# Gate and value products of a SwiGLU block in three float32r passes over split operands, in place of float32 products

## The chip, the cores and the metric

The kernel runs on one core of one Trainium2 chip. The metric is the device time of one execution in microseconds, the median of the runs; lower is better. Engine names are those of the profile: PE (TensorE matmuls), PEld (its weight loads), DVE (VectorE), ACT (ScalarE), POOL (GpSimd), SP (SyncE, which here issues most DMA transfers).

## The reference

A causal depthwise convolution of seven taps (softmax weights, one set for each of eight heads of 24 channels) over `x` of 8 x 4096 x 192, then a SwiGLU feed-forward block with RMS norm over the 32768 tokens, all in float32. The feed-forward weights arrive as float64.

```python
out = np.einsum('hk,bskhg->bshg', softmax(weight), windows_of(x_pad))      # K = 7 taps, causal
x = out.reshape(B * S, D)                                                  # 32768 x 192
rms = np.sqrt(np.mean(x * x, axis=-1, keepdims=True) + 1e-06)
xn = x / rms * rms_g
g = xn @ w_gate                                                            # 192 -> 1536
silu = g * (1.0 / (1.0 + np.exp(-g)))
val = xn @ w_val                                                           # 192 -> 1536
return (silu * val @ w_out).astype(np.float32)                             # 1536 -> 192
```

## The kernel before

**Tiling.** The tokens go in 32 pairs of 1024 (`PT`), each of two groups of `T` = 512. The 192 channels are three blocks of 64 (`KP`), the 1536 features twelve blocks of 128 (`FC`), in four units (`NU`) of three (`NF`). A normalized input tile `xb` holds each block of 64 channels twice: the lower 64 partitions meet the gate's weights, the upper 64 those of the value. A product of one channel block with one feature block and one token group is two matmul instructions of 64 x 512, one per half of the array, which run at the same time into two PSUM banks. All products are in float32.

**Gate and value.** Pair 0 uses plain products (`plain`, matmul on L1052): 2 groups x 12 feature blocks x 3 channel blocks = 72. From pair 1 on a scheme with sums of operands needs 60 in place of 72: 15 per unit. `XSUM` (L67) gives eleven sums of inputs (`x_sum`, L701, into `xc`), `WSUM` (L71) nineteen sums of weights, made once (`w_sums`, L361, on POOL). `CHAIN` (L749) lists the products; `Unit.product` (L792) issues them on L794. Results are carried from bank to bank: `Unit.do` (L800) has copies out (S), copies into a new bank (F; `copy`, L741, with L743 on ACT and L745, L747 on DVE), additions (D, N, C, R, L810 to L826), the silu on ACT (G, L839) and the product of silu and value (M, L846, on POOL or DVE). The hidden blocks go into `ht`.

**Output.** The product with `w_out` uses seven forms of a Strassen kind (`OUTS`, L865) with six steps each: 42 steps per pair, each of six tiles of 128 x 32 weights, four of which run side by side in the columns of the array (`Pair.tile`, L933, matmul on L934). The sums of hidden blocks that the forms need are made on POOL (`Pair.sum`, L954, instructions on L962), 24 per pair. Pair 0 has plain output products (`outer`, L1086, matmul on L1093). DVE turns the results in 32 x 32 blocks (L949) and SP stores them.

**Ahead of the pair.** The convolution of pair p + 2 runs during pair p, in three parts of 512 columns that stand in PSUM banks (`part_tap`, L460: a first tap on ACT, L468, six on DVE, L476). Then square, sum, power and scaling (`square` to `scale`, L489 to L532), a way through DRAM that turns the tile (`place`, L657, SP) and the fetch into `xb` (`fetch_part`, L690, SP).

**Order.** From pair 1 on the order of all instructions is written out by hand in `ORDER` (L90). A word such as `p2` emits the next two steps of PE; `VR1.0.0` is an action on DVE, with A for ACT, G for POOL, D for DMA issues; a word that ends in `-` belongs to the pair before. Each engine, and SP's queue too, takes its instructions in this order. The start, up to the end of pair 0, is laid out by `START`, `LATER` and times given to `put` (L1178 to L1261).

Of the kernel before, what the change touches and what calls it, by code (L numbers as in the profile page):

```python
# [11 lines left out]
F32 = mybir.dt.float32  # L12
AF = mybir.ActivationFunctionType
# [6 lines left out]
def kernel(  # L20
# [45 lines left out]
    XOP = (5, 6, 9, 0, 15, 14, 4, 7, 13, 10, 2, 11, 12, 8, 3)  # L66
    XSUM = (  # L67
        (0, 1, 4), (1, 2, 6), (2, 0, 6), (9, 3, 5), (3, 3, 8), (4, 7, 15), (5, 4, 15), (6, 5, 7),
        (7, 0, 1), (8, 1, 2), (9, 8, 15),
    )  # L70
    WSUM = (  # L71
        (9, "sub", 5, 2), (9, "sub", 9, 8), (10, "sub", 1, 4), (10, "add", 7, 10),
        (11, "sub", 1, 8), (7, "sub", 7, 11), (11, "sub", 4, 11), (12, "add", 1, 6),
        (4, "sub", 12, 4), (5, "sub", 5, 4), (5, "add", 3, 5), (13, "sub", 2, 6),
        (13, "add", 0, 13), (14, "sub", 3, 12), (3, "sub", 6, 3), (0, "add", 0, 3),
        (3, "sub", 3, 2), (6, "neg", 6, 6), (8, "neg", 8, 8),
    )
    WAT = (7, 9, 2, 0, 1, 4, 5, 11, 14, 6, 10, 12, 8, 3, 13)

    SPAN = 1509
    ORDER = (  # L90
        "p2 GX4- VT11- p2 AS40.0.0 GX9- AS40.1.0 p2 AF0.1.0 AF0.0.0 p2 VC.0.0 Dload- p2",
        "VC.1.0 AS41.0.0 VS41.1.0 p2 AS00.1.0 VS00.0.0 p2 Vbc- VD5.0.0 Gmul- p2 VD5.1.0",
        "AS42.0.0 VS42.1.0 AS51.1.0 p2 AS51.0.0 VR1.0.0 p2 VR1.1.0 VR0.0.0 p2 AF2.0.0 VN.1.0",
        "AG0.0.0 p2 VR0.1.0 AF3.0.0 Dplace- AF3.1.0 p2 GM0.1.0 VR2.0.0 p2 VR2.1.0 AS44.1.0",
        "AS44.0.0 VR5.1.0 p2 AG2.0.0 VR3.0.0 p2 GM2.1.0 AS40.0.1 VR3.1.0 AS40.1.1 p2 VR5.0.0",
        "AG4.0.0 p2 VM4.1.0 AF0.0.1 AG5.0.0 VF0.1.1 p2 AG1.0.0 VS41.0.1 GM5.1.0 p1 AS41.1.1",
        "p1 VC.0.1 AG3.0.0 p1 VC.1.1 p1 GM3.1.0 VS00.0.1 p2 AS42.0.1 VS42.1.1 AS00.1.1 GS3.0",
        "p2 VD5.0.1 p1 VD5.1.1 p1 AS51.0.1 GS1.0 VR1.0.1 AS51.1.1 p2 VR1.1.1 AF2.0.1 GS3.1 p2",
        "AF2.1.1 VR0.0.1 AG1.0.1 p1 VR0.1.1 p1 GM1.1.1 VF3.0.1 AF3.1.1 p2 AG0.0.1 VR2.0.1 p1",
        "VR2.1.1 p1 GM0.1.1 AS44.0.1 AS44.1.1 VR5.0.1 p2 GS2.0 VR5.1.1 p2 AS40.0.2 VR3.1.1",  # L100
        "AS40.1.2 p1 VR3.0.1 GM1.1.0 p1 AG4.0.1 AG3.0.1 p1 VM4.1.1 p1 GM3.1.1 VF0.0.2 AF0.1.2",
        "p2 AS41.0.2 VS41.1.2 p1 AG5.0.1 p1 VC.0.2 GM5.1.1 p1 VC.1.2 p1 AS00.0.2 AS00.1.2 p2",
        "GS1.1 AS42.1.2 AS42.0.2 p2 VD5.0.2 GS3.2 p1 VD5.1.2 p1 AS51.0.2 VR1.0.2 AS51.1.2 p2",
        "GS2.1 VR1.1.2 AF2.0.2 p2 AF2.1.2 VR0.0.2 GS1.2 AG1.0.2 p1 VR0.1.2 p1 AG0.0.2 VF3.0.2",
        "GM1.1.2 p1 AF3.1.2 p1 VR2.0.2 AG2.0.1 p1 VR2.1.2 p1 AS44.0.2 GM2.1.1 AS44.1.2 p2",
        "VR3.0.2 AG2.0.2 GS2.2 p1 VR3.1.2 p1 AS40.0.3 VR5.0.2 AS40.1.3 p2 GM2.1.2 AG4.0.2",
        "VR5.1.2 AG3.0.2 p1 VM4.1.2 p1 AF0.0.3 GM0.1.2 p2 AF0.1.3 VS41.0.3 AS41.1.3 p2",
        "GM3.1.2 AG5.0.2 VC.0.3 p1 VC.1.3 p1 AS00.1.3 GS3.3 AS00.0.3 p2 VS42.0.3 AS42.1.3 p2",
        "GS1.3 VD5.0.3 p1 VD5.1.3 p1 AS51.0.3 GM5.1.2 VR1.0.3 AS51.1.3 p2 VR1.1.3 AF2.0.3 p2",
        "GS2.3 AF2.1.3 VR0.0.3 AG1.0.3 p1 VR0.1.3 p1 GS4.2 VF3.0.3 AF3.1.3 p2 AS44.0.3",  # L110
        "VS44.1.3 p1 GM1.1.3 p1 VR5.1.3 p1 VR5.0.3 p1 Acv0_1 VR3.0.3 AG5.0.3 p1 Vcv1_1 Acv0_2",
        "GM5.1.3 p2 VR3.1.3 AG0.0.3 p2 AG3.0.3 Vcv1_2 DfetA GS3.4 p1 AG4.0.3 p1 VR2.0.3 p2",
        "Acv0_0 Vcv2_2 GM3.1.3 p2 VM4.1.3 p2 Vcv2_1 Ac1 GS3.5 p1 AG2.0.3 p1 Vcv3_1 p2 GS1.4",
        "Vcv3_2 p2 Vcv1_0 p2 GS2.4 p1 Vcv2_0 p2 Vcv4_1 p1 As7 GS1.5 DfetB Dst0- p1 VR2.1.3 p2",
        "Vcv5_1 p1 GM0.1.3 p1 Vcv3_0 p2 Vcv6_1 p1 GS2.5 p1 Vcv4_0 p2 Vcv4_2 GS4.0 p2 Vcv5_0",
        "p2 GS4.1 p1 Vcv6_0 p2 Vcv5_2 Ac2 p1 GX0 p1 Vcv6_2 p2 VM2.1.3 Asq p2 GS4.4 p4 VX3 p1",
        "GS4.3 p4 VX6 p1 GX2 p2 VC22 p2 VX1 p2 GS4.5 VT22 p2 Vred p2 GX8 p3 GX7 p2 VC21 p2",
        "VT21 Gpow p2 VX5 p2 VX10 p2 VT12 p1 Dst1 p1",
# [15 lines left out]

    def load_heads(p, b, t0):

        t = x_sb[p] = xs.tile([P, TB + HALO, GS], F32, name="xh")
        if p == 1:
            nc.gpsimd.tensor_copy(out=t[:, 0, 0:1], in_=x0[:, NJ + HALO - 1, 0:1])

        def get(dst, tb, h, dims, r):
            row = x[b, t0 + tb * TB + r - HALO, h * GS :]
            src = bass.AP(
                tensor=row.tensor, offset=row.offset, ap=[dims, [D, TB + HALO - r], [1, GS]]
            )
            nc.sync.dma_start(out=dst, in_=src)

        first = 0
        if t0 == 0:
            nc.gpsimd.memset(t[0:H, 0:HALO, :], 0.0)  # L150
            get(t[0:H, HALO:, :], 0, 0, [GS, H], HALO)
            first = 1
        for h in range(H):
            get(t[first * H + h :: H], first, h, [TB * D, P // H - first], 0)
# [28 lines left out]
    ps = [psum.tile([P, T], F32, name=f"ps{i}") for i in range(8)]  # L183
# [17 lines left out]
    NW = 15  # L201
    wf = [cst.tile([P, NW, P], F32, name=f"wf{u}") for u in range(NU)]
# [13 lines left out]
    def load_in(u, q):  # L216
# [9 lines left out]
    NT = 11  # L226
    few = NT - 6
    early = work.tile([P, 3, NJ * D], F32, name="early")
    kept = [early[:, i].rearrange("p (j d) -> p j d", d=D) for i in range(3)]
    kept = itertools.cycle(kept)  # L230
    flat3 = early[:].rearrange("p i n -> p (i n)")
    NK = FC // 2
    held = [flat3[:, k * T : (k + 1) * T] for k in range(9)]
    more = work.tile([P, 2, T], F32, name="more")
    diff, both, rest = held[0:NK], held[NK:], [more[:, i] for i in range(2)]
    nw = 4 * (FC // 2) * (D // 2)
    tw = x0[:].rearrange("p j d -> p (j d)")[:, 0:nw].rearrange(
        "p (i k d) -> p i k d", i=4, k=FC // 2
    )
    tl6 = [work.tile([P, 3, T], F32, name=f"tls{i}") for i in range(2)]  # L240
    tiles = [work.tile([P, T], F32, name=f"tile{i}")[:] for i in range(few)]
    room = [t[:].rearrange("p j d -> p (j d)") for t in tl6]
# [102 lines left out]
    xb = cst.tile([P, 2, KP, T], F32, name="xb")  # L345
    NX = len({s[0] for s in XSUM})
    xc = cst.tile([P, NX, T], F32, name="xc")
    spare = xc[:].rearrange("p i t -> p (i t)")
# [12 lines left out]
    def w_sums(u):  # L361
        t = wf[u]
        for i, (d, op, a, b) in enumerate(WSUM):
            if op == "neg":
                nc.gpsimd.tensor_scalar(
                    out=t[:, d, :], in0=t[:, a, :], scalar1=-1.0, scalar2=None, op0=ALU.mult
                )
            else:
                nc.gpsimd.tensor_tensor(
# [3 lines left out]
            if i % 4 == 3:  # L373
                yield
        yield


    def convert_in(u):

# [930 lines left out]
```

## Time and profile before

| | |
|---|---|
| time, median of 3 runs | 2594.28 us (2593.07 to 2600.1) |
| span of the profiled execution, first to last instruction | 2591.8 us |
| instructions | 60798 |
| matmul records, all / on L794 / on L934 | 23872 / 7440 / 15624 |
| gate and value of one pair, output of one pair (chain) | 51.92 us, 27.44 us |
| plain products of pair 0 (L1052), output of pair 0 (L1093) | 62.17 us, 31.31 us |
| granted TensorE clock | 1.000 |
| HBM read, written | 83.84 MB, 49.55 MB |

How to read it: the span is cut into groups of instructions by line, engine and tile, each with its count, busy time and mean duration. Records of one engine can overlap, and then a group's busy time divided by its count is less than the mean. The chain of waits is followed back from the last instruction: at each step to what released it, or to the instruction before it on its engine. A stretch of the chain on one line with no other line between is time in which that engine never waited.

### The profile page before, as it was taken

To read this page: it belongs to the slowest core of one execution; us is meant where nothing else is said; L and a number is where in the kernel's file an instruction comes from. 1 tells how busy PE (TensorE), PEld (TensorE's weight loads), DVE (VectorE), ACT (ScalarE), POOL (GpSimd) and SP (SyncE) were. 2 spreads that over 40 slices of the span, in tenths; PEclk is the share of its full clock that TensorE was granted. 3 is DMA by queue.
4 is the path that set the end of the run, shared out by engine and by line. 5 is a ranking of instruction groups with operands and counts; after the bars stand their busy time and mean duration, and the time that the engine had idled before them with its cause. 6 is when DMAs were issued, how large, how long until landed. Compare 5 with 4: busy or idle time off the path is not lost.

```text
span 2591.8 us, 60798 instructions
## 1 busy us (share of the span) xinstructions
PE 2580.5 (100%) x23872; PEld 1778.0 (69%) x23872; DVE 2298.8 (89%) x3681; ACT 1553.5 (60%) x2825; POOL 2190.6 (85%) x1791
## 2 busy tenths in 40 slices
PE   9999999999999999999999999999999999999999
PEld 6876666767667666676666676666766666766667
DVE  8898898988989989989889899899898898988975
ACT  6576555675555765556755557655566555676554
POOL 4898888988889888898888898888988888988877
PEclk9999999999999999999999999999999999999999
DMA  6232332222331323322223313233222233122210
GB/s 145 57 57 33 63 64 52 44 45 51 63 63 38 57 33 64 63 49 47 45 51 64 62 38 55 36 63 63 46 49 45 52 63 58 37 56 40 50 44 14
DMA packets 512397, 137.33 MB, mean 53 GB/s; under 512 B 483950, under 2 KB 486510, under 8 KB 512110
## 3 DMA queue, kind: packets, MB, share of 16 engines
q1 hardware_dynamic: 508364, 132.53, 27.2%
q8 instruction: 187, 3.06, 0.5%
q10 hardware_dynamic: 3746, 0.92, 0.2%
q14 instruction: 100, 0.82, 0.1%
HBM read 83.84 MB, written 49.55 MB: 51 GB/s over the span
## 4 chain that ended last, share of the span: by engine, by line
PE 99%; DVE 0%; issue 0%; DVEq 0%
PE ps L794 62%; PE ps L934 33%; PE ps L1052 2%; PE ps L1093 1%; DVE xb L647 0%; DVE wf L338 0%; DVE xc L333 0%; DVE o_sb L949 0%; DVE xc L298 0%; DVE xc L303 0%; DVE xc L306 0%; DVEq L1305 0%
## 5 line engine op out<-in xcount | busy, mean ns | idle before, releaser
L794 PE MATMUL ps<-xc,wf 64*128 64x512 f32 x4960 | 1214.0, 591 | 0.0
L794 PEld LDWEIGHTS ps<-xc,wf 64*128 64x128 f32 x4960 | 681.3, 186 | 375.3 <-issue 176.7
L794 PE MATMUL ps<-xb,wf 64*128 64x512 f32 x2480 | 679.7, 591 | 0.0
L743 ACT ACTIVATE tile<-ps 128x512 f32<-128x512 f32 x678 | 391.1, 593 | 389.0 <-PE ps L794 295.3
L743 ACT ACTIVATE tls<-ps 128x512 f32<-128x512 f32 (+1 forms) x562 | 323.5, 589 | 438.6 <-PE ps L794 222.0
L846 POOL TENSOR_TENSOR ht<-ht,tile 128x512 f32<-128x512 f32 x329 | 418.9, 1275 | 141.0 <-ACT tile L839 65.2
L794 PEld LDWEIGHTS ps<-xb,wf 64*128 64x128 f32 x2480 | 353.9, 187 | 182.9 <-issue 93.6
L846 POOL TENSOR_TENSOR ht<-ht,tls 128x512 f32<-128x512 f32 x260 | 330.6, 1274 | 86.4 <-ACT tls L839 38.8
L743 ACT ACTIVATE ps<-ps 128x512 f32<-128x512 f32 (+1 forms) x589 | 336.0, 580 | 87.9 <-PE ps L934 32.6
L962 POOL TENSOR_TENSOR early<-ht 128x512 f32<-128x512 f32 x279 | 354.8, 1276 | 4.9
L476 DVE SCALAR_TENSOR_TENSOR ps<-xh,tp,ps 128x512 f32<-128x512 f32 x450 | 320.3, 748 | 4.0 <-ACT ps L468 1.8
L934 PE MATMUL ps<-ht,wo_sb 128*32 128x128 f32 (+2 forms) x5208 | 318.5, 380 | 0.0
L934 PEld LDWEIGHTS ps<-ht,wo_sb 128*32 128x32 f32 x5208 | 233.9, 110 | 81.7 <-POOL ht L846 23.5
L934 PE MATMUL ps<-ht,x 128*32 128x128 f32 (+2 forms) x4464 | 250.7, 379 | 0.0
L826 DVE TENSOR_TENSOR tile<-ps,tile 128x512 f32<-128x512 f32 x349 | 237.4, 683 | 10.2 <-PE ps L794 5.0
L962 POOL TENSOR_TENSOR ht<-ht 128x512 f32<-128x512 f32 x186 | 239.0, 1285 | 4.9
L826 DVE TENSOR_TENSOR ht<-ps,tile 128x512 f32<-128x512 f32 x328 | 222.5, 680 | 6.5 <-ACT tile L743 6.5
L934 PEld LDWEIGHTS ps<-ht,x 128*32 128x32 f32 x4464 | 184.3, 110 | 61.3
L839 ACT ACTIVATE tile<-tile 128x512 f32<-128x512 f32 x349 | 214.5, 625 | 0.0
L826 DVE TENSOR_TENSOR ht<-ps,tls 128x512 f32<-128x512 f32 x292 | 199.0, 681 | 6.8 <-ACT tls L743 3.6
L826 DVE TENSOR_TENSOR tls<-ps,tls 128x512 f32<-128x512 f32 x271 | 184.9, 683 | 17.0 <-PE ps L794 13.8
L934 PE MATMUL ps<-early,x 128*32 128x256 f32 (+2 forms) x3348 | 196.0, 379 | 0.0
(149 smaller groups left out, 3278.1 us busy)
## 6 DMA issues: line engine op xcount, KB each, us to landing
xb<-xd SPq DMA_DIRECT2D x120, 384.0 KB
xd<-yn SPq DMA_DIRECT2D x244, 96.0 KB
xh<-in_x_dram SPq DMA_DIRECT2D x192, 105.0 KB
out_dram<-o_sb SPq DMA_DIRECT2D x122, 96.0 KB
out_dram<-o_sb SPq DMA_DIRECT2D x60, 128.0 KB
xh<-in_x_dram SPq DMA_DIRECT2D x56, 98.4 KB
out_dram<-o_sb SPq DMA_DIRECT2D x122, 32.0 KB
ht<-in_moe_w_gate_dram SPq DMA_DIRECT2D x12, 192.0 KB
```

The source lines that it names most:

```text
L476: nc.vector.scalar_tensor_tensor(out=dst, in0=xk, scalar=w, in1=at, op0=ALU.mult, op1=ALU.add)
L743: nc.scalar.activation(out=dst, in_=src, func=AF.Copy, scale=float(s))
L794: nc.tensor.matmul(out=self.new(v, h, True) if first else self.old(v, h), lhsT=wf[self.u][HALF[h], WAT[i], :], rhs=x_op(XOP[i])[HALF[h]], ...
L826: nc.vector.tensor_tensor(out=self.hv(v) if h else t[:], in0=self.old(v, h), in1=t[:], op=plus(s))
L839: nc.scalar.activation(out=t[:], in_=src[:], func=AF.Silu)
L846: engine[eng].tensor_tensor(out=self.hv(v), in0=src, in1=t[:], op=ALU.mult)
L934: nc.tensor.matmul(out=self.bank(b)[i * Q : (i + 1) * Q, at : at + n], lhsT=left, rhs=cols, start=fresh, stop=True, skip_group_check=True, ...
L962: engine[eng].tensor_tensor(out=dst, in0=a, in1=b, op=op)
L1052: nc.tensor.matmul(out=bank(h, bks[h])[:], lhsT=wf[u][HALF[h], AT[h][k] * NF + f, :], rhs=xb[HALF[h], g, k, :], start=(k == 0), stop=(k == ...
L1093: nc.tensor.matmul(out=bank(h, bks[h])[:, w : w + D], lhsT=hts[f // NF][HALF[h], g, f % NF, j * P : (j + 1) * P], rhs=wo_sb[HALF[h], f, :] ...
```

## The change

Gate and value from pair 1 on are computed otherwise; the output's 42 steps stay.

- **Split operands.** Each weight operand is split once into three parts: the high bits (a mask, `HIGH`), 4096 times the rest, and their difference divided by 1 + 2^-12 and rounded to float32r. Each input operand is split per pair: rounded to float32r (`n`), the rest (`l`), and 2^-12 times the first less the second (`d`). The sum of the three products of like parts is the whole product, but for a factor 1 / (1 + 2^-12), which `factor` puts right in the norm. So each product is three passes of float32r matmuls, two instructions each (`Pair.product`).
- **Which products.** Feature blocks go in six block pairs j. For j = 0, 2, 4 (`FORM`) a Strassen form needs 7 products for two of the three channel blocks and 4 plain ones for the third: 11. For j = 1, 3, 5 there are 12 plain ones. In all 69 per pair of token groups. Four sums of inputs (`x_sum`) replace eleven.
- **Pair 1** has 72 plain float32 products, since the split weights are made during it and before it (`prepare`, words `W` in `FIRST`; it writes them to DRAM, `wd`).
- **Weights from DRAM.** The split weights do not stay in SBUF. A ring of ten slots of 128 x 384 is filled by SP, 45 loads of 196.6 KB per pair; a slot is loaded anew after the last product that uses it (`ring_load`).
- **PSUM** is taken as four double banks (`duo`), so that one instruction of 1024 columns copies gate and value at once (f1, f3, f4, f5).
- **The rest of the order.** Sums of hidden blocks: 18 of 24 on DVE, six on POOL (before, all on POOL). The product of silu and value is always on DVE. The convolution of pair p + 1 runs during pair p, in SBUF, with 1536 columns an instruction. Some DMA issues go to ACT's queue. `ORDER` is new, with `FIRST` for the window of pair 1; a word with `+` belongs to the next pair. `LINE` is the order of PE's steps: a word such as `P1.0` or `Aa.1` is a gate and value product of block pair 0 or 1, `o4.5` an output step.

```diff
-    XSUM = (
...
-    WSUM = (
...
+    SPLIT = 2.0**-12
+    HIGH = 0xFFFFF000
+    FORM = (1, 0, 1, 0, 1, 0)
...
+    ORDER = (
+        "p12- As7- Acv0+ Ac2- Vl.1 Vcv1+ p10- Gh4.0- Vh4.5- Vh4.1- Vcv2+ Vh4.3- Vcv3+ VC22-",
+        "Vcv4+ Gh4.4- VT22- Vl.0 p8- Gh4.2- VT11- VC21- VT21- p3- p1 Af1.0 p1 VT12- p1 Vcv5+",
+        "p5 Af3.0 Aga.0 Vcv6+ Vma.0 p1 Vf4.0 Gl.4 p5 Asq+ Aga.1 Agb.1 Vred+ Vmb.1 Vma.1 p1",
+        "Gpow+ Vf5.0 Agc.0 p2 Vmc.0 Vbc+ p1 Agc.1 Agd.0 Vmd.0 p2 Agb.0 Gmul+ p1 Vmc.1 Vmb.0",
...
+        "Vd.1+",
+    )
...
+    LINE = (
+        "P1.0 Aa.1 P5.0 Q1.0 P2.0 Ba.1 P6.0 Ea.1 Ab.1 Eb.1 Bb.1 Q2.0 P7.0 P3.0 Ac.1 Ec.1 Bc.1",
...
+        "Bd.5 o1.0 o1.3 o1.1 o1.5 o1.4 o1.2 o7.0 o7.2 o7.1 o7.4 o7.3 o7.5 o2.5 o6.3 o6.4 o6.5",
...
+    duo = [psum.tile([P, 2, T], F32, name=f"ps{i}") for i in range(4)]
+    ps = [duo[i % 4][:, i // 4, :] for i in range(8)]
...
+        s = (1.0 + SPLIT) ** -2 if p > 1 else 1.0
...
+    def prepare(o):
...
+        high = parts[:, 0]
+        nc.vector.tensor_scalar(
+            out=high.bitcast(U32), in0=src.bitcast(U32), scalar1=HIGH, scalar2=None,
+            op0=ALU.bitwise_and,
+        )
+        nc.scalar.activation(out=w4, in_=src, func=AF.Copy, scale=1.0 / SPLIT)
+        yield
+        nc.vector.scalar_tensor_tensor(
+            out=parts[:, 1], in0=high, scalar=-1.0 / SPLIT, in1=w4, op0=ALU.mult, op1=ALU.add
+        )
+        yield
+        nc.gpsimd.tensor_tensor(out=e, in0=parts[:, 1], in1=high, op=ALU.subtract)
+        yield
+        nc.scalar.activation(
+            out=parts[:, 2].bitcast(F32R), in_=e, func=AF.Copy, scale=1.0 / (1.0 + SPLIT)
+        )
+        yield
+        nc.sync.dma_start(out=wd_of[o][:, js], in_=st.rearrange("p (j x) -> p j x", j=NP)[:, js])
...
+    def ring_load(slot):
+        n = next(taken)
+        q, (j, o) = 2 + n // len(pieces_of), pieces_of[n % len(pieces_of)]
...
+        r = (j * NW + o) * P
+        nc.sync.dma_start(out=ring[0][:, slot, :], in_=wd[r : r + P, :])
...
+    def split(act, g, eng):
+        src, high = operand(g), split_of(g, 0)
+        e = engine.get(eng)
+        if act == "n":
+            copy(eng, high.bitcast(F32R), src)
+        elif act == "l":
+            e.tensor_tensor(out=split_of(g, 1).bitcast(F32R), in0=src, in1=high, op=ALU.subtract)
+        else:
+            nc.vector.scalar_tensor_tensor(
+                out=split_of(g, 2).bitcast(F32R), in0=high, scalar=1.0 + SPLIT, in1=src,
+                op0=ALU.mult, op1=ALU.subtract,
+            )
...
+        def product(self, w, j):
...
+            for q in range(3):
+                left = ring[0][:, slot, q * P : (q + 1) * P].bitcast(F32R)
+                right = split_of(g, q)[:, i, :].bitcast(F32R)
                 for h in range(2):
+                    nc.tensor.matmul(
+                        out=self.both(j, c)[:, h, :], lhsT=left[HALF[h]], rhs=right[HALF[h]],
+                        start=(first and q == 0), stop=True, skip_group_check=True,
+                    )
+            left_of[key] -= 1
+            if left_of[key] == 0:
+                ring_load(slot)
...
+            if act == "f1":
+                self.open((j, "b"), True)
+                copy(eng, self.both(j, "b"), self.both(j, "a"))
+            elif act == "f3":
+                copy(eng, s5, self.both(j, "c"))
+            elif act in ("f4", "f5"):
...
+                nc.vector.tensor_tensor(
+                    out=self.both(j, c), in0=self.both(j, "b"), in1=s5, op=ALU.add
+                )
+            elif act[0] == "g":
...
+                nc.scalar.activation(
+                    out=tt[:, t, :], in_=self.both(j, c)[:, 0, :], func=AF.Silu
+                )
+            elif act[0] == "m":
...
+                nc.vector.tensor_tensor(
+                    out=self.hv(j, "abcd".index(c)), in0=self.both(j, c)[:, 1, :],
+                    in1=tt[:, t, :], op=ALU.mult,
+                )
+            elif act[0] == "h":
+                self.h_sum(int(act[1]), j, eng)
```

Words of `ORDER` that the prediction names: `ga` to `gd` silu, `ma` to `md` its product with the value, `h1` to `h4` sums of hidden blocks, `cv0` to `cv6` taps, `sq`, `red`, `pow`, `bc`, `mul` the norm, `pl` the way into DRAM, `ft` the fetch of x, `ld` loads of x, `st` stores, `s7`, `c1`, `c2`, `C22`, `C21` carries of output banks, `T11` to `T22` the turns.

## The prediction, on record before the changed kernel ran

> **What bounds the kernel now.** I read the chain of waits first, then its stretch of two steady pairs, then busy time by stretch. On the page, the chain is PE and almost nothing else:
>
> ```profile
> span 2591.8 us, 60798 instructions
> PE 2580.5 (100%) x23872; PEld 1778.0 (69%) x23872; DVE 2298.8 (89%) x3681; ACT 1553.5 (60%) x2825; POOL 2190.6 (85%) x1791
> PE ps L794 62%; PE ps L934 33%; PE ps L1052 2%; PE ps L1093 1%; DVE xb L647 0%; DVE wf L338 0%; DVE xc L333 0%; DVE o_sb L949 0%; DVE xc L298 0%; DVE xc L303 0%; DVE xc L306 0%; DVEq L1305 0%
> ```
>
> PE works without a gap: L794 (gate and value) and L934 (output) alternate. The chain in order of time (start, length, what), at the beginning and in two later pairs:
>
> ```profile
> 32.40 62.17 PE ps L1052 x271
> 94.58 31.31 PE ps L1093 x380
> 126.37 51.72 PE ps L794 x239
> 178.09 27.44 PE ps L934 x337
> ```
>
> ```profile
> 1157.98 51.92 PE ps L794 x240
> 1209.90 27.44 PE ps L934 x337
> 1237.34 51.92 PE ps L794 x240
> ```
>
> A pair is 51.92 + 27.44 = 79.36 us. The 51.92 are 60 products of 512 columns, 0.865 us each, both halves of the array at once. L1052 agrees: 72 products in 62.17 us, 0.863 each. The model of the whole is 126.4 (start and pair 0) + 79.2 (pair 1) + 30 x 79.36 + 4.9 (from the last matmul to the end) = 2591.3 against a span of 2591.8. The median of the runs, 2594.28, is 2.5 us above that span; I add these 2.5 at the end.
>
> How far are the others from being the bound? Busy time by stretch (PE, PEld, DVE, ACT, POOL, clock, DMA share, GB/s):
>
> ```profile
> 1158.00:1209.90 51.90, 51.90 (x244) 32.83 (x248) 45.58 (x75) 41.50 (x77) 41.70 (x33) 1.00 0.23 35
> 1209.90:1237.30 27.40, 27.40 (x507) 21.00 (x506) 25.95 (x40) 6.60 (x11) 26.79 (x23) 1.00 0.37 83
> 43.00:46.00 3.00, 3.00 (x17) 1.44 (x14) 3.00 (x4) 0.90 (x2) 2.40 (x4) 1.00 1.07 372
> 1291.00:1293.00 2.00, 2.00 (x42) 1.62 (x38) 2.00 (x4) 1.37 (x3) 2.00 (x2) 1.00 0.93 245
> ```
>
> DVE has 71.5 of 79.3 us, POOL 68.5. The last two rows are the DMA engines when full: 372 GB/s for rows of 1536 bytes (the loads of w_out), 245 GB/s for rows of 2048 bytes (xb).
>
> **The price of a pass.** The change turns 60 float32 products into 3 x 11 + 3 x 12 = 69 products of three float32r passes, 207 passes, each of two instructions (one per half of the array). No row shows a float32r instruction. From above: if it costs what a float32 one does, 0.865 us a pass. From below: the page counts 7440 matmul records on L794 for 60 x 2 x 31 = 3720 instructions, so a float32 instruction is two records, each with its own weight load, and a record of 512 columns takes 0.4327 us. The new operands are cut to the bits that one part holds (HIGH, and a rounding write), so one record per instruction: 0.4327 at most. Is the moving side cut too? L1093 says what a column costs in a float32 record: 31.31 us for 384 records of 192 columns, two at a time, is 0.163 per 192, 0.85 ns a column, the same as 0.4327 / 512. PE does nothing between, so the price is in the columns, and if the moving side also goes in two parts, one part is half: 51.92 / 240 = 0.2163 us. I take 0.2163, since both operands of the change hold one part where both of the rows hold two; 0.4327 and 0.865 stay as upper ends.
>
> The Trainium skill (FP8 and Floating Point Precision, TensorE Precision Notes) says that true FP32 is four passes, high and low of both operands, and that a reduced read truncates to FP22. By that a pass is 0.865 / 4 = 0.216, and the four-fold product of this trace agrees; float32r itself no run here shows.
>
> **Can the weights be loaded that fast?** A pass needs two loads of 64 x 128 per 0.2163 us, 0.108 us each; now it is two per 0.43.
>
> ```profile
> L794 PEld LDWEIGHTS ps<-xc,wf 64*128 64x128 f32 x4960 | 681.3, 186 | 375.3 <-issue 176.7 <-ACT ps L743 31.6 <-ACT tile L743 13.1
> ```
>
> One load takes 186 ns, so 414 loads a pair would be 77 us end to end. But L1093 has the same shape and got 384 of them into 31.31 us, 0.082 each: they overlap. So I cost the loads at nothing; without that cover they are a rival below.
>
> **PE after.** Gate and value: 207 x 0.2163 = 44.8 us. Output: the same 42 steps of six tiles, 27.44. Pair: 72.2, a gain of 7.1, for pairs 2 to 31. Pair 1 is done in plain float32, 72 products at L1052's 62.17 instead of 51.72: 10.4 lost. Start, pair 0 and end keep their work on the path. Sum: 126.4 + 62.2 + 27.4 + 30 x 72.2 + 4.9 = 2387.5; with the 2.5, **2390**.
>
> **What the cover must do in 72.2 us.** Durations are those of the rows (683 ns for 512 columns of PSUM, 550 for 384, so 1.04 ns a column).
>
> DVE, per pair: 24 products with the silu 16.4; six f4/f5 of 1024 columns at 1.22, 7.3; six taps of 1536 columns at L452's 1.82, 10.9; 18 h sums at 0.69, 12.4; eight splits of 1024 at 1.22, 9.8; x1 and n.3 1.7; red and bc 2.4; C22, C21 1.1; four turns 2.9. That is 64.9 in 78 instructions. Records overlap:
>
> ```profile
> 1165.25 0.68 DVE L826 TENSOR_TENSOR tls<-ps,tls 128x512 f32<-128x512 f32 x1
> 1165.85 0.68 DVE L826 TENSOR_TENSOR ht<-ps,tile 128x512 f32<-128x512 f32 x1
> 1166.44 0.68 DVE L826 TENSOR_TENSOR tls<-ps,tls 128x512 f32<-128x512 f32 x1
> ```
>
> 0.68 long, but started every 0.60, so 78 x 0.085 = 6.6 comes off: 58 us. The rest is a surcharge for POOL:
>
> ```profile
> L705 DVE TENSOR_TENSOR xc<-xb x34: 685/1770/1779, 117.5 to 2486.6; 128x512 f32<-128x512 f32 x34
> L705 POOL TENSOR_TENSOR xc<-xb x90: 1257/1278/1739, 192.2 to 2506.2; 128x512 f32<-128x512 f32 x90
> ```
>
> (ns, min/median/max.) A DVE sum with both inputs in SBUF takes 0.685 at best and 1.77 beside a POOL sum. The change moves 18 of 24 h sums from POOL to DVE and adds the splits, 33 such instructions, but POOL keeps only 19.5 us of SBUF work (nine sums 11.5, two splits 5.1, the scaling 2.9). If all of it meets them: 19.5 x 1.08 / 1.28 = +16.5, DVE 75. DVE is in such an instruction 34 us of 72, so I take half: 58 + 8 = 66 of 72, 91%, where it now has 90%.
>
> The Trainium skill (SBUF — State Buffer, Who interferes with whom) says that a DVE instruction with two SBUF inputs and a GpSimd one that reads SBUF exclude each other for the whole instruction. The 1.77 agrees; by that rule the surcharge is still at most the 19.5 us that POOL holds the port, 77.5 for DVE.
>
> ACT: 24 silus 14.4, six copies of 1024 columns 6.2, six long ones (cv0, sq, four n) 7, small 1.5, ten DMA issues at some 0.5: 34 us. It hides. POOL: some 22, no longer near anything.
>
> DMA: 45 pieces of 196.6 KB, 8.8 MB a pair from DRAM. At 372 GB/s a piece is 0.53 us, 24 us a pair, beside the 27% of 79 = 21 us that the queues take now (page, part 3). SP issues 45 + 19 transfers at 0.43 us (the o_sb loads) to 0.64 (xb: 1.28 for two), 31 us. By LINE, a piece is asked for when its slot's last product is done, at least nine products, 5.8 us, before its own. The tightest place: between the first x fetch (26.7 us into the products) and the use of piece (5,3) at 42.2 stand nine pieces, three fetches of 524 KB at 245 GB/s and one load of x (0.8): 4.8 + 6.4 + 0.8 = 12 us, plus some 1.5 before a first packet, against 15.5. It fits. SP also holds Spl.0, which waits for POOL's scaling; pieces behind it wait too, and have some 2 us to spare.
>
> **Waits added on PE.** f1 must copy a bank between P1 and Q1 (three steps, 1.95 us; the copy 1.03 plus two hand-overs of 0.1 and the drain of 0.16): nearly nothing. f4, f5 and the four double banks come free with 0.5 to 1 us to spare by the same sums, so an engine a little late shows on PE. Bounds per pair: nothing, as now with DVE equally full, and 5.3 (DVE's 77.5). I take 0.5, near the lower end because the nearest row is the present pair with none: 15 us. Forecast **2405**.
>
> **Rivals.**
> 1. Weight loads set the pace. In L794 the loads of the two halves start 0.147 us apart in places; if they can't come closer, a pass is 0.294, a pair 60.9 + 27.4 = 88.3, the time 2390 + 30 x 16.1 = **2873**, slower. It decides from a pass of (51.92 - 10.4 / 30) / 207 = 0.249 us on. For: twice as many loads per column as in any row of L794. Against: L1093's 0.082. The dearer float32r stream (0.4327) would give 117 a pair, 3730; it is the same mechanism, the price of a pass.
> 2. DVE becomes the bound: 75 to 77.5 a pair, 2390 + 30 x 2.8 to 5.3, **2475 to 2550**. For: 33 instructions that POOL can stretch, and PSUM that only four double banks hold. Against: POOL falls from 68 to 22 us.
> 3. Weights come late: at 245 GB/s a piece is 0.8 us, the tight place needs 14.4 + 1.5 in 15.5 us, and an SP queue held by a wait adds to it; at 1 us a pair, **2420**. For: SP issues in order. Against: rows of the very shape at 372 GB/s.
> 4. It gives nothing: DVE's 75 with half of the 7.8 us that it idles per pair now is 79, **2590**.
>
> **How the numbers follow.** Forecast 0.53 (its own range 2385 to 2430), late weights 0.09, DVE bound 0.17: faster by over 0.3%, which is about what a measurement can tell from no change, 0.79. Rival 4 as no change 0.02. Slower 0.19: rival 1 0.14, rival 4 with more idle 0.05. The range goes from 2380 (no wait at all and a little less in the start) to 2550, the end of the DVE case; what lies beyond is 0.21.
>
> **What would show it.** Right: the chain 99% PE, with some 44.8 us of products per pair and 27.4 of output; 414 matmul records a pair, one per instruction; DVE busy near 90%, POOL near 30%; DMA near 60% and 120 GB/s more. Wrong: products longer than 51.6 us a pair (a dear pass, seen in records over 0.25 us apart with no wait), gaps on PE ended by DVE or ACT (rival 2) or by the ring's DMA (rival 3), h sums at 1.7 us.

## The result and the profile after

The changed kernel takes **3437.34 us** (median of four runs, 3432.37 to 3440.9) against 2594.1 us of the kernel before: **slower, ratio 1.3248, 95% interval 1.3229 to 1.3266**. Forecast were 2405 us, with a range up to 2550. One execution of all those told of here stands apart, the fourth of e1 below: 11073.5 us at a granted clock of 0.22, of unknown cause; without it e1's median is 2697.7 us in place of 2699.3. The page of the profiled execution, the lines that answer to those of before, with the row of the granted clock:

```profile
span 3430.5 us, 68984 instructions
PE 2606.5 (76%) x29140; PEld 2086.3 (61%) x29140; DVE 2020.2 (59%) x2575; ACT 946.4 (28%) x1349; POOL 793.7 (23%) x552
PEclk9798888898888898888988888988889888889889
PE 57%; DMA 35%; SPq 5%; DVE 1%; issue 1%; POOL 1%; ACT 0%; ACTq 0%; DVEq 0%; POOLq 0%
PE ps L898 30%; PE ps L922 24%; DMA xb<-xd 19%; DMA ring<-wd 15%; SPq L784 2%; PE ps L1069 2%; SPq L149 1%; PE ps L870 1%; SPq L633 1%; DMA wd<-part 1%; DVE y L439 1%; PE ps L1110 0%; SPq L767 0%; POOL ht L222 0%; SPq L232 0%
```

No engine is full; a third of the chain is two transfers, the fetch of the input (`xb<-xd`, L633) and the ring (`ring<-wd`, L784). The products are now L898, the output is L922. The chain in order of time, one pair and the beginning of the next:

```profile
1488.77 23.09 DMA xb<-xd
...
1517.03 14.26 DMA ring<-wd
...
1531.33 5.49 PE ps L898 x20
1536.82 27.64 PE ps L922 x336
1564.46 29.58 PE ps L898 x254
...
1594.23 23.27 DMA xb<-xd
```

The output still takes 27.6 us. The products run for 29.6 us and then stand still until the input's fetches have landed. A row of 23 us runs from the issue of a fetch to its landing, and two fetches share that time: SyncE's first and ScalarE's are issued within a microsecond (1487.86 and 1488.77), and their 256 packets of 4096 bytes move together, in 21.0 us (median of 28 pairs). The third moves alone, in 12.5 us. I had given each 2.1 us. From one pair's first product to the next one's are 105.0 us (mean of the trace; forecast 72.7). The waits, engine, line, releaser: total, times, longest, of the engines and then of SyncE's queue:

```profile
PE ps L898 <- DMA ring<-wd: 735.5, 58, 20.3
...
DVE tt L826 <- DMA xb<-xd: 505.5, 30, 18.9
```

```profile
SPq L784 <- DMA xb<-xd: 674.2, 30, 24.5
```

PE waits for the ring, but the ring waits for the fetch: once a pair SyncE holds the next ring load until a fetch has landed, 22.5 us in the mean and 24.5 at most. What the fetch is doing in that time stands in the DMA view of 1480 to 1520 us, 40 slices of 1 us, with the mean share of the 16 transfer engines in tenths and what they moved:

```profile
DMA  8389989799511111111111111111111018899976
GB/s 191 89 286 210 264 215 215 241 327 312 191 45 66 57 49 49 57 49 49 57 49 49 53 53 49 53 53 49 49 53 45 8 15 273 230 283 343 296 139 185
```

For some 20 us the share is one tenth, at 45 to 66 GB/s. In most of the slices on either side, where ring loads run, it is 0.7 to 0.9, at 200 GB/s and more. The fetch's packets, those of 4096 bytes, take some 160 ns each, and two of them are under way at a time: 2 of 16 engines is 0.125, and two times 4096 bytes in 162 ns are 51 GB/s. So the first theory: **the new form of the fetch, whose access pattern has an outermost dimension of two, runs on two transfer engines.** Rivals: its zero step; the ring's own traffic; a dear float32r pass.

### The profile page after: what moved, and what is told of

Read it like the earlier page. It is cut to its first block, busy times and chain, and to the rows that moved or that the text cites. A ratio compares the mean times of both kernels' runs of the same rounds, so it can differ in the third digit from the quotient of the medians.

```text
span 3430.5 us, 68984 instructions
## 1 busy us (share of the span) xinstructions
PE 2606.5 (76%) x29140; PEld 2086.3 (61%) x29140; DVE 2020.2 (59%) x2575; ACT 946.4 (28%) x1349; POOL 793.7 (23%) x552
## 4 chain that ended last, share of the span: by engine, by line
PE 57%; DMA 35%; SPq 5%; DVE 1%; issue 1%; POOL 1%; ACT 0%; ACTq 0%; DVEq 0%; POOLq 0%
PE ps L898 30%; PE ps L922 24%; DMA xb<-xd 19%; DMA ring<-wd 15%; SPq L784 2%; PE ps L1069 2%; SPq L149 1%; PE ps L870 1%; SPq L633 1%; DMA wd<-part 1%; DVE y L439 1%; PE ps L1110 0%; SPq L767 0%; POOL ht L222 0%; SPq L232 0%
## 5 line engine op out<-in xcount | busy, mean ns | idle before, releaser
L898 PE MATMUL ps<-part,ring 64*128 64x512 f32 x12420 | 1560.3, 412 | 735.6 <-DMA ring<-wd 735.5
L898 PEld LDWEIGHTS ps<-part,ring 64*128 64x128 f32 x12420 | 1304.4, 199 | 980.1 <-issue 519.3
L972 ACT ACTIVATE tt<-ps 128x512 f32<-128x512 f32 x744 | 444.5, 600 | 1545.8 <-PE ps L898 1202.0
L979 DVE TENSOR_TENSOR ht<-ps,tt 128x512 f32<-128x512 f32 x744 | 502.3, 688 | 580.8 <-ACT tt L972 577.4
L922 PE MATMUL ps<-ht,wo_sb 128*32 128x256 f32 (+2 forms) x6696 | 438.2, 382 | 7.4 <-DVE tt L996 7.4
L922 PE MATMUL ps<-ht,x 128*32 128x384 f32 (+2 forms) x6696 | 426.9, 381 | 19.8 <-ACT tt L666 19.8
L922 PEld LDWEIGHTS ps<-ht,wo_sb 128*32 128x32 f32 x6696 | 309.9, 111 | 102.1 <-issue 10.5
L439 DVE SCALAR_TENSOR_TENSOR y<-xh,tp,y 128x1536 f32<-128x1536 f32 x186 | 369.1, 1985 | 1.1
L922 PEld LDWEIGHTS ps<-ht,x 128*32 128x32 f32 x6696 | 298.6, 110 | 108.9 <-ACT tt L666 20.0
L826 DVE TENSOR_TENSOR tt<-xb 128x512 f32<-128x512 f32 x30 | 21.0, 701 | 505.5 <-DMA xb<-xd 505.5
L966 DVE TENSOR_TENSOR ps<-ps,tt 128x1024 f32<-128x1024 f32 x180 | 221.9, 1233 | 145.5 <-PE ps L898 81.3
L812 POOL TENSOR_TENSOR part<-tt,part 128x1024 fp32r<-128x1024 f32 x60 | 172.3, 2872 | 76.6 <-DVE part L668 73.8
L949 DVE TENSOR_TENSOR ht<-ht 128x512 f32<-128x512 f32 x248 | 169.4, 693 | 8.0 <-PE ps L922 6.8
L826 POOL TENSOR_TENSOR tt<-xb 128x512 f32<-128x512 f32 x30 | 38.4, 1280 | 536.2 <-DMA xb<-xd 536.2
L922 PE MATMUL ps<-hs,x 128*32 128x128 f32 (+2 forms) x2232 | 150.2, 381 | 0.3 <-ACT tt L666 0.3
## 6 DMA issues: line engine op xcount, KB each, us to landing
xh<-in_x_dram SPq DMA_DIRECT2D x104, 105.0 KB
xh<-in_x_dram ACTq DMA_DIRECT2D x88, 105.0 KB
```

What stands on the lines that cost most here:

```text
L439: nc.vector.scalar_tensor_tensor(out=y, in0=xk, scalar=w, in1=y, op0=ALU.mult, op1=ALU.add)
L812: e.tensor_tensor(out=split_of(g, 1).bitcast(F32R), in0=src, in1=high, op=ALU.subtract)
L826: engine[eng].tensor_tensor(out=dst, in0=a, in1=b, op=op)
L898: nc.tensor.matmul(out=self.both(j, c)[:, h, :], lhsT=left[HALF[h]], rhs=right[HALF[h]], start=(first and q == 0), stop=True, skip_group_c ...
L922: nc.tensor.matmul(out=self.acc(b)[i * Q : (i + 1) * Q, at : at + n], lhsT=left, rhs=cols, start=fresh, stop=True, skip_group_check=True, ...
L949: engine[eng].tensor_tensor(out=dst, in0=a, in1=b, op=op)
```

## The experiments

A time with an interval or a ratio is a median of several executions, any other that of a single one. The interval is that of the ratio to the kernel before, measured beside it (2592.8 to 2594.1 us throughout).

**e1: the fetch by rows.**

```diff
-        src = bass.AP(tensor=row.tensor, offset=row.offset, ap=[[0, 2], [PT, HP], [1, PT]])
-        queue(eng).dma_start(out=rb[:, k].rearrange("p g t -> p (g t)"), in_=src)
+        for rows in (LOW, UPP):
+            queue(eng).dma_start(out=rb[rows, k].rearrange("p g t -> p (g t)"), in_=row)
```

> The fetch of x into xb goes as two transfers of 64 rows (as in the kernel before) in place of one whose source has a zero step of 2 in front; nothing else differs from the changed kernel. Theory A, the fetch: its outermost dimension of 2 puts it on two of 16 DMA engines, it takes 23 us, the x sums and the weight ring's loads queue behind it. Then here xb lands within some 4 us, the waits for xb and most of those for the ring go, the clock stays near 1.0, a pair is 207 x 0.2267 + 27.4 = 74.4 us with some 0.5 of waits: 2460 to 2490. Rival B, the ring: 8.8 MB of weights a pair is itself too much or too late; then the waits for the ring stay and the time is above 2800. Rival C, the clock: float32r passes themselves pull the granted clock below 0.95; above 2600 with PE full.

2699.3 us, ratio 1.0408 (1.0387 to 1.0429); mean granted clock 0.976 against 0.876. The same bytes in two transfers of 64 rows save 738 us: the fetch is the cause of most of the loss. But the kernel is still slower than before and more than 200 us above what I expected, so that something else is late too. A fetch's packets now move in 3.2 us (median of 77, 2.5 to 4.4). The chain:

```profile
1558.01 29.67 PE ps L898 x258
...
1588.39 5.89 DMA xb<-xd
...
1594.96 4.16 DMA ring<-wd
```

By the trace's semaphores, ScalarE's two fetches (issued at 1587.86 and 1588.39) carry numbers 100 and 102, and SyncE's next fetch carries the same two: SyncE stands idle from 1587.1 until they have landed, and issues at 1593.72, with seven ring loads behind it. PE waits 2.4 to 4.8 us a pair for them (97.6 us in all), and behind 22 of these 29 waits the clock is at half for 3.4 or 6.8 us.

**e2: two in front, without a zero step.** e1 with each transfer of 64 rows written as two times 32 (even rows, odd rows, which permutes the channels).

```diff
+            src = bass.AP(
+                tensor=row.tensor, offset=row.offset, ap=[[PT, 2], [2 * PT, HP // 2], [1, PT]]
+            )
```

> As e1, two transfers of 64 rows without any zero step, but each reads first the even and then the odd rows of its block, so that the outermost dimension of the source is 2 again (the channels come permuted, so the numbers computed are those of permuted channels). If the outermost dimension of 2 is what binds (theory A), the fetch is as slow as in the changed kernel: 3300 to 3500. If the zero step itself is what binds, it is as fast as e1: 2460 to 2490.

3462.16 us. No row is read twice in a transfer here, and the loss is back: the size of the outermost dimension decides, not the zero step. Nor is it that the pattern has three dimensions: the fetch of the kernel before (`fetch_part`, `(k p) t -> p k t`) has three too, with 64 rows in front, and the prediction's row of it shows a share of 0.93. The Trainium skill (DMA: Bandwidth & Descriptors, Why a DMA increments its semaphore by 16 and not by 1) says that a transfer is spread over the largest number up to 16 that divides the slowest dimension of both patterns; two in front gives two engines. The share of a tenth and e2 agree, and its rules for kernel authors name this very pattern. I had not set this rule against the diff.

**e3: the form alone, in the kernel before.**

```diff
-        for rows in (LOW, UPP):
-            nc.sync.dma_start(
...
+        for k in range(KP):
+            at = xd[k * HP : (k + 1) * HP, g * T : (g + 1) * T]
+            src = bass.AP(tensor=at.tensor, offset=at.offset, ap=[[0, 2], [PT, HP], [1, T]])
+            nc.sync.dma_start(out=xb[:, g, k], in_=src)
```

> The kernel before with the changed kernel's form of fetch: per channel block one transfer of 128 rows of 2048 bytes with a zero step of 2 in front. No ring, no float32r. Theory A: six transfers of 256 KB per pair on two engines, at 0.08 to 0.14 us a row of 2 KB 5 to 9 us each in place of about 1, so 30 to 54 us for the six where there are some 10 before the next products: 2900 to 3400. Rival B (it is the ring that binds, the fetch only waits with it): 2594, within 1 per cent.

2958.77 us, 365 more than before, without a ring, a float32r product or any other part of the change. Its chain has the same row, and its DMA view (1290 to 1310 us) the same shares:

```profile
1288.94 19.59 DMA xb<-xd
```

```profile
DMA  2111111111111121111145112711184342111110
```

**e4: twice the weight loads.** e1 with each float32r matmul cut in two of 256 columns.

```diff
+                for a in (0, 256):
                     for h in range(2):
```

> e1 with each float32r matmul of 512 columns cut into two of 256 with the same weights, so twice the weight loads for the same columns. A pass of the changed kernel takes 0.2267 us where streaming was forecast at 0.2163. If the columns set the pace with a small fixed cost per matmul, a pass of 256 takes 0.107 + 0.013 = 0.12 us, a pair 30 x 69 cells' cost grows by 207 x 0.013 = 2.7 us: 2540 to 2580. If the weight loads set the pace (the next load of a half starts only when its matmul starts, and takes 0.223), a pass of 256 takes 0.22 too, a pair is 93 + 27 = 121 us: above 3800.

2757.35 us, 58 more than e1 or 1.9 us a pair (the expected times, 2.7 us a pair, counted on a faster e1), for 414 more matmuls and loads a pair. Had the loads set the pace, the products would have doubled. Rival 1 of the prediction falls: the price is in the columns, but for a small one of each matmul. By this difference it is an estimated 9 ns a pass (1.9 us / 207).

**e5: all three fetches on SyncE**, against the shared semaphores of e1.

```diff
-        "Aft.1+ Vmb.3 Af1.4 ...
+        "Sft.1+ Vmb.3 Af1.4 ...
```

> e1_fetch_rows, with the second of the three fetches issued by SyncE instead of ScalarE (one word of the order). Theory held order: in e1 the first fetch of SyncE carries the semaphore that ScalarE's fetch carried just before, waits until that has landed (SyncE idle 1587.2 to 1593.7 us) and holds the ring loads behind it; with all three on one queue SyncE's waits for xb<-xd fall from 165 us to under 40, the products' waits for the ring from 97.6 us to under 25, the half clock behind them goes too, and the time is 2530 to 2580 us. Rival, too many bytes in the tight place: the same bytes move in the same place, the wait only changes its name, and the time stays at 2670 to 2710 us.

2736.13 us, ratio 1.0543 (1.0525 to 1.056): slower than e1. The wait I meant did go: SyncE's waits for `xb<-xd` fell to 45 us and PE's for the ring to 11.7. Another came in its place. Chain, and PE's largest wait:

```profile
1607.93 6.05 DMA xb<-xd
...
1614.00 8.01 DMA xb<-xd
...
1622.08 0.69 DVE tt L826
...
1623.48 1.24 DVE ps L966
...
1624.86 10.76 PE ps L898 x72
```

```profile
PE ps L898 <- DVE ps L966: 134.1, 29, 5.6
```

The fetches now leave one behind the other between ring loads; the second lands at 1622. VectorE's first sum of the next pair's input (`x1`, L826) waits for it, and behind that sum stands f4 (L966), which a product needs. So to take this wait away alone gains nothing in this order; what it cost in e1 is not settled by that (see e11).

**e6: the ring loaded once.** e1 without the later ring loads.

```diff
+        if n < NSLOT:
+            nc.sync.dma_start(out=ring[0][:, slot, :], in_=wd[r : r + P, :])
```

> e1_fetch_rows with each of the ten ring slots loaded once and never again (the products then use the weights of the first pieces; the 1350 loads of 192 KB that fill the ring become 10). This is the floor for a ring that is never late. If late ring loads and the half clock behind them are the whole excess of the steady pairs (80.8 us against 74.4), the time is 2500 to 2540 us, with the start unchanged. If the matrix engine waits for something else in these places (a split operand, a bank), it stays above 2600 us.

2506.88 us, as expected; PE does not wait for the ring, 74.7 us a pair. So the later ring loads cost e1 192 us, by their bytes, their issues and their places in SyncE's queue together, and nothing else in the steady pairs costs anything to speak of: the two terms of a pair without a gap are 74.66 (below).

**e7: no new input.** e5, and the eight loads of 96-byte rows a pair left out after the fourth pair.

```diff
+        if p > 4:
+            x_sb[p] = last[0]
+            return
```

> e5_fetch_one_queue, and the input of the pairs after the fourth is not loaded again (their convolution runs on what the input tile holds; eight loads a pair of rows of 96 bytes are left out). Theory held order: the input loads only fill the time beside the ring, so the gain on e5 is at most 10 us. Rival, too many bytes in the tight place: these loads take every transfer engine for about a microsecond each, so that leaving them out gains 40 us or more on e5.

2736.02 us, the same as e5: these loads are not what is in the way there.

**e8 and e9: the sums later**, in e5 and in e1.

```diff
-        ... Gh1.3 Sft.2+ p1 Vf4.4 p2 Aga.4 Vx1+",
-        "Vma.4 Gx3+ Gx2+ p3 Vf5.4 p2 Agc.4 Aga.5 Gx4+ Vn.3+ p1 Vmc.4 An.4+ Agd.4 Ald.1++",
...
+        ... Gh1.3 Sft.2+ p1 Vf4.4 p2 Aga.4",
+        "Vma.4 p3 Vf5.4 p2 Agc.4 Aga.5 p1 Vmc.4 Agd.4 Ald.1++ Gh3.3 Ald.2++ Agb.4 Ald.3++",
+        "Vma.5 Vmd.4 Vx1+ Gx3+ Gx2+ Gx4+ Vmb.4 p5 Vn.3+ An.4+ Gl.3+ p4 Vd.4+ An.0+ Ald.4++ Agb.5",
```

> e5_fetch_one_queue with the sums of the next pair's input (four sums and the first splits) moved some six products later in the order, nothing else. In e5 the ring is on time (11.7 us of waits in all), and each pair loses 4.7 us because VectorE stands 6.8 us in front of its first sum, which waits for the fetched input, with the update of a bank that the products need behind it. Theory order: with the sum behind that update nothing is late, the wait of the products for VectorE falls from 134 us to under 20, and the time is 2510 to 2560 us, below before. Rival, too many bytes in the tight place: the fetched input is then late for the splits at the pair's end or the ring is late again, and the time is 2620 us or more.

> e1_fetch_rows (second fetch on ScalarE) with the same sums moved later as in e8. Theory order: the ring loads stay behind SyncE's fetch that waits for ScalarE's, so that the products' wait for the ring stays near 97 us and the time at 2670 to 2710 us. If the late sum was the cause in e1 too, and the semaphore was not, it falls below 2600 us.

2790.66 us (ratio 1.0761, 1.0735 to 1.0786) and 2791.41. Both miss. The largest wait of PE in e8, and its chain ahead of a pair's output:

```profile
PE ps L922 <- DVE ht L979: 103.8, 33, 5.2
```

```profile
1582.92 2.34 DVE part L814 x2
1585.26 0.61 DVE ht L979
...
1585.92 25.97 PE ps L922 x288
```

The splits (L814), pushed back, now stand in front of the last product with the silu (L979), which the output needs. In e9 the same wait is 84.3 us, and the one for the ring stays, at 94.7. VectorE's order is tight on both sides: the input must come earlier.

**e10: the input earlier.**

```diff
-        "p1 Af1.2 Spl.0+ p2 Spl.1+ Spl.2+ Af3.2 Spl.3+ Spl.4+ Vh1.0 p4 Agd.1 Spl.5+ Vf4.2",
...
+        "p1 Af1.2 Spl.0+ Spl.2+ Spl.4+ Spl.6+ p2 Af3.2 Apl.1+ Apl.3+ Vh1.0 p4 Agd.1 Apl.5+",
+        "Apl.7+ Vf4.2 Vmd.1 p1 p4 Aga.2 Vma.2 Vf5.2 Agc.3 Sft.0+ p4 Agd.2 Vh3.0 Vh1.1 Agb.2",
```

> e5_fetch_one_queue with the next pair's input sent off earlier: the eight stores right behind the scaling that makes them (four on each queue, where they stood between ring loads), and the three fetches some five products earlier; the sums stay where they were in e5. What e5 and e8 left: the input arrives too late for its first sum, and a later sum is too late for the pair's end, so the arrival must come forward. In e5 the scaling ends at 1594.5 us, the stores leave until 1604.3, the fetches until 1622.3, and SyncE issues without a break in between at some 0.65 us each. With stores gone by 1599 and fetches landed by about 1612, ahead of the first sum at 1614, the wait of 4.7 us a pair goes: 2530 to 2600 us. Rival, SyncE and the transfer engines have no room in this stretch whatever the order: ring loads that now stand behind the fetches come late instead, 2650 us or more.

2663.08 us, ratio 1.0267 (1.025 to 1.0285): 73 less than e5 and the best with all of the work, but short of what I expected. VectorE is hardly late any more; PE waits 70.4 us for the ring, in 68 small waits.

**e11 and e14: a quarter of the ring's bytes**, in the order of e1 and in that of e10.

```diff
+        e = KP * P if n < NSLOT else P * KP // 4
+        nc.sync.dma_start(out=ring[0][:, slot, 0:e], in_=wd[r : r + P, 0:e])
```

> e1_fetch_rows with every ring load after the first ten cut to a quarter of its bytes (rows of 384 bytes for 1536; the products use three parts of the weights that are out of date). As many issues on SyncE, the same semaphores and order, 30 MB instead of 265 MB over the ring's loads, roughly. If the bytes of the ring make the transfers late, the time falls to the floor that e6 gave, 2500 to 2540 us. If SyncE's issues one behind the other and its waits for landed transfers do, it stays at 2640 us or more.

> e10_input_earlier with the ring loads after the first ten cut to a quarter of their bytes (weights partly out of date). Bytes theory: with the order of e10 only the ring's bytes are left, and the time falls to 2505 to 2530 us. Order theory: the issues and the waits for landed transfers are as in e10, and it stays above 2590 us.

e11 takes 2619.23 us, between the two expectations: of e1's 192 us, 80 go with three quarters of the bytes (a quarter of 265 MB is 66 MB, not 30). With few bytes left, PE still waits 63.2 us for the ring, and SyncE 142.3 us ahead of its fetches for `xb<-xd`, which points to the shared semaphores of e1's order, not to bytes. e14 takes 2511.53, the floor of e6. In the order of e10 the bytes are all that is left. By stretch, e10 and then e14 (PE, PEld, DVE, ACT, POOL busy, clock, DMA share, GB/s):

```profile
1622.00:1630.00 8.00, 7.38 (x66) 5.62 (x62) 4.84 (x7) 2.44 (x4) 0.00 (x0) 1.00 0.95 233
1630.00:1638.00 8.00, 7.16 (x64) 6.13 (x64) 5.63 (x10) 3.00 (x5) 0.00 (x0) 1.00 1.01 299
1638.00:1646.00 8.00, 7.18 (x62) 5.50 (x58) 3.91 (x5) 3.70 (x5) 3.06 (x3) 1.00 1.06 251
```

```profile
1622.00:1630.00 8.00, 8.00 (x74) 6.62 (x72) 6.51 (x9) 3.40 (x6) 0.00 (x0) 1.00 0.70 159
1630.00:1638.00 8.00, 8.00 (x74) 6.60 (x72) 4.20 (x8) 3.32 (x6) 2.53 (x2) 1.00 0.84 213
1638.00:1646.00 8.00, 8.00 (x74) 6.61 (x72) 7.28 (x10) 4.04 (x7) 4.71 (x3) 1.00 0.32 67
```

In e10 the transfer engines are full for 24 us, at 233 to 299 GB/s, and PE has gaps; in e14 they are not, and it has none. Over e10's steady pairs as a whole (419.6 to 2565.9 us) the share is 0.66, at 163 GB/s: room is short in this stretch, not over the pair. A ring of more slots, whose loads could run ahead of the stretch, was not tried.

**e12 and e13: transfers spread; weights prepared later.**

```diff
-    SOON = 35
+    SOON = 24
```

(e13 alone, with eleven more `W` in `FIRST`; e12 moves stores, fetches and input loads by a few words.)

> e10_input_earlier with its transfers spread: two ring loads between the stores, the second and third fetch two and four products later, and the input loads of ScalarE behind its last copy for the splits, which in e10 waited behind them. If it is the order that still costs e10 its 2.4 us of ring waits a pair, these halve and the time is 2590 to 2635 us; if bytes do, it stays at 2640 to 2670 us.

> e12_spread, and eleven of the 35 steps that prepare split weights move from the output of pair 0 into the gate products of pair 1. If these steps, each a chain over four engines with a store of 0.6 to 1.2 MB behind it, make the start late (the plain products of pair 1 end at 219 us in e1, against the 189 us that the prediction's working puts there), the start gains 10 to 25 us and the rest is as e12. Rival, the two buffers and the stores set the pace of the preparation wherever it stands: within 5 us of e12, or later.

e12: 2675.69 us (ratio 1.0306, 1.0262 to 1.0351). Against e10 this is no clear change, and no gain; that no order at all would help, it does not show. e13: 2682.15 (1.035, 1.0335 to 1.0365); pair 2's products begin at 274.9 us against 263.2 in e12, so that moving these steps does not shorten the start.

**e15: two thirds of the ring's bytes.** As e14, with `e = ... else 2 * P`.

> e10_input_earlier with the third part of each piece left out of the ring loads after the first ten (rows of 1024 bytes for 1536; the third pass uses parts that are out of date). In e10 the transfer engines are full for some 24 us of a pair (1622 to 1646), with about 25 pieces in them; a third of these bytes is 4 to 5 us, just the excess of 4.8 us a pair over e14. If capacity is short by that much, the time is 2510 to 2560 us. If the ring asks for too much all along, it falls in proportion to the bytes, to about 2595 us.

2538.2 us: of the 152 us between e10 and e14, a third of the bytes brings back 125. The transfers are short by little in this place.

**e16, e17, e18: the missing third made on the core.** e10 with two thirds loaded, and this ahead of each piece's first product (e17; on GpSimd in e18; e16 has a difference on GpSimd and a scaled copy on ScalarE):

```diff
+            nc.vector.tensor_tensor(
+                out=part[:, 2].bitcast(F32R), in0=part[:, 1], in1=part[:, 0], op=ALU.subtract
+            )
```

> e10_input_earlier, with two thirds of each piece loaded and the third part made on the core, four steps of the matrix engine ahead of its use: a difference on GpSimd and a scaled copy on ScalarE, of 128 columns each, 45 of each a pair. All of the computation is there. GpSimd has 24 of 75 us busy and ScalarE 28, so some 15 us more on each fit; what they may cost is hand-overs in front of a product. Theory, the ring's bytes are the last cost: the time is that of e15 and up to 40 us more, 2520 to 2590 us, below before. Rival, the two engines stand in their order in front of a piece that has not landed and hold the silus: 2620 us or more.

> e10_input_earlier, two thirds of each piece loaded, the third part made by one difference of 128 columns on VectorE four steps ahead of its use; the factor that ScalarE applied in e16 goes into the third split of the input, whose instruction stays one. All of the computation is there. VectorE is 81 per cent busy in e14, 60.6 of 74.8 us a pair; 45 instructions of some 0.2 us (a quarter of the 0.69 of a sum of 512 columns, and a little) make it 70. If nothing new waits, the time is that of e15, 2538 us; I expect 2540 to 2585 us, below before. Rival: VectorE is too full, or stands in front of pieces that have not landed, and the matrix engine waits for it, 2600 us or more.

> e17_third_on_vector with the difference on GpSimd, some 0.43 us each. In e16 ScalarE waited 912 us for GpSimd's differences, and GpSimd's sums of hidden blocks waited 627 us for the matrix engine in front of them. If GpSimd's own queue made e16 late, this stays above 2700 us; if the second hand-over to ScalarE did, it falls below 2600 us.

2995.15 us (ratio 1.1553, 1.1535 to 1.157), 2816.25 (1.0857, 1.0842 to 1.0872) and 2703.79. e16 and e17 come out where their rivals put them, e18 just above the 2700 us that were to speak for GpSimd's own queue. In e16, other than its expectation says, the scratch of the difference lies over the sums of the output weights, so that the output products run on overwritten values, and what part of its time is due to this the runs do not tell; so e18 does not settle what made e16 late. The instruction itself, in e17 and in e18:

```profile
L898 DVE TENSOR_TENSOR ring<-ring 128x128 fp32r<-128x128 f32 x1350 | 471.7, 384 | 106.3 <-DMA ring<-wd 101.2 <-PE ps L914 0.2
```

```profile
L898 POOL TENSOR_TENSOR ring<-ring 128x128 fp32r<-128x128 f32 x1350 | 783.0, 605 | 363.5 <-DMA ring<-wd 267.5 <-PE ps L914 93.8 <-POOL ring L898 0.3
```

The means, 384 and 605 ns, mix two cases. The medians are 282 ns on VectorE, where I had put 0.2 us, and 460 on GpSimd. But 112 of the 1350 on VectorE take 0.4 to 2.5 us, all with an instruction of GpSimd beside them, as only 94 of the other 1238 have. To this come 3.4 us a pair in which VectorE waits for a piece with everything else behind it. With the difference on GpSimd, PE waits 68.9 us for the result. No version that does all of the work came below the kernel before.

## Why the prediction was wrong

The miss is 3437 - 2405 = 1032 us. It splits by kernels: 738 from the fetch's two engines (after to e1), 192 from the ring's later loads (e1 to e6), 102 between e6 and the forecast.

- **The step that failed** is the one on DMA: "three fetches of 524 KB at 245 GB/s", and with it "It fits". The three fetches took 33.5 us of transfers a pair (21.0 for two together, 12.5 for the third) instead of 6.4, and the ring's loads stood behind them. The rate came from rows of the old fetch, whose pattern has 64 rows in front; that the new one has a two in front, the prediction does not weigh. e1, e2 and e3 show that this one edit costs 738 us here and 365 in the kernel before.
- **The same step failed a second time.** Even with the fetch on 16 engines the tight place does not fit: 372 GB/s for a piece held with nothing beside it, while ring, fetches, stores and input loads together move 233 to 299 GB/s when the engines are full (e10). Rival 3, weights late, had the right mechanism at 1 us a pair; it is 4.7 in e10 (79.6, less 74.9 in e14) and 6.2 in e1 (80.9 - 74.7), and 30 in the changed kernel (105.0), behind the fetch.
- **The price of a pass** was right in kind and low in size. e14 has a pair without a gap:

```profile
1604.10 47.22 PE ps L899 x414
1651.32 27.44 PE ps L923 x337
```

  47.22 us for 207 passes is 0.228 each, one record per instruction, against 0.2163: 2.4 us a pair, 73 of the 102 us. The 9 ns that e4 suggests for cutting a pass would be most of the 12 by which the two differ, but no run separates them. The price stays below the 0.249 from which rival 1 decides. That the moving side would be halved too was a choice between 0.2163 and 0.4327 with no row of float32r to go by. The prediction's "four-fold product of this trace" is no support for it, since the trace shows two records for a float32 instruction, not four passes.
- **Weight loads** at no cost: right (e4). **Output** at 27.44: right to the digit. **Waits** of 0.5 us a pair: in e6 a pair is 74.72, its two terms 74.66, so under 0.1, which takes 13 us off.
- **VectorE, ScalarE, GpSimd** (rivals 2 and 4): in e14's pair from 1604.10 to 1678.76 VectorE is busy 63.3 us where I put 66, and ScalarE 28.6 for 34. (The 60.6 of e17's expectation is taken from the whole span, start and end included.) No rival was needed here; but e5, e8 and e17 show how little it may be late.
- **The start** was too short. Pair 2's products begin at 305 us, and at 256 in e14, where I had 216. The 40 us lie in two places of e14: pair 0's output takes 58.4 us for 31.3 (92.5 to 150.9) and pair 1's 41.7 for 27.4 (214.6 to 256.3). 25 us of it are PE's waits behind evacuations on ScalarE and VectorE, and for 34 us the clock is at half. e13 did not shorten it. Which step makes it long stays open. Passes, start and waits, 73 + 40 - 13, are 100 of the 102 us.
- **The clock** was taken as 1. It falls with the waits: 0.876 in the changed kernel, 0.976 in e1, 0.993 in e6 and e14, with the same passes in all. The Trainium skill (TensorE: Matmul & The Clock Gate, Part 1) says that at least one idle window of about 3.4 us halves the clock. e1's stretches at half, of 3.4 and 6.8 us, agree with the window's length. How long a wait must be, e1 does not show: a wait of 2.4 us had half a clock behind it, one of 3.3 had none.

So the idea of the change was worth 86 us (2593 to 2507) with its weights at hand, and its traffic took more than that: 156 us in the best order found.

## What to carry to other kernels

Compare a new transfer's access pattern with the old one dimension by dimension, the outermost first: a two in front moved a fetch at 49 GB/s, and its 512 KB took 10.5 to 12.5 us of transfer where the same bytes by rows took 3.2. Price a stretch of transfers by the rate that they reach together there, not by the best rate of the largest alone. When a wait is taken away in an order written by hand, look at once for the instruction that is next behind the late data: of the four edits e5, e8, e9 and e10, three moved the wait to another engine and lost time.

## What the runs showed of the hardware that I had not expected

A float32r pass of 512 columns, two halves of the array at once, takes 0.228 us, 5% more than a quarter of a float32 product's 0.865. A difference of 128 columns took 282 ns on VectorE (median) where one of 512 takes 682, and up to 2.5 us when GpSimd worked beside it; a mean hides this. Fetches whose pattern has a two in front had two packets under way at a time, also when two such fetches, issued by different engines, ran at once: together they moved at some 49 GB/s for 21 us, with the share of all 16 engines at one tenth, while SyncE's queue waited for them.
